# Turning the second half's normalised tokens on VectorE and through DRAM instead of on TensorE

## The chip, the core and the metric

One core of a Trainium2 chip. The metric is the device time of one execution in microseconds (us); the median of the runs is used. Engines, as the profile names them: PE is TensorE (PEld its weight loads), DVE is VectorE, ACT is ScalarE, POOL is GpSimd, SP is SyncE, whose queue (SPq) issues the DMAs.

## The reference

S = 2048 tokens of D = 576 values, all in 32 bits. `x` is normalised per token, and the result is the input plus the sum of two branches:

```python
xn = _layernorm(x)                       # (x - mean) / sqrt(var + 1e-5)
return x + A(xn, wqkv, wo) + B(xn, w1, b1, w2)
# A: 32 heads of 18; each token attends to itself and 7 earlier tokens, 2 apart; then @ wo
# B: h = xn @ w1 + b1; h * tanh(softplus(h)); @ w2      (576 -> 4608 -> 576)
```

## The kernel before, in words

**Halves, blocks, tiles.** The tokens are worked in two halves of 1024 (hf 0 and 1), each of two blocks (b 0 and 1), each of four tiles (jj) of 128 tokens. Tile n = 4 b + jj of a half holds 128 tokens that lie 8 apart, one per partition.

**Numbers in two parts.** Matmuls run on float32r. Every operand is split into a high part (a cast, on ScalarE) and a low part (the value minus the high part, on VectorE or POOL), and a product is made of three matmuls: high by high, high by low, low by high.

**Normalised and turned.** For a product over D the tokens must lie with D on the partitions. In the second half a tile goes this way: `x_load` (L103) loads it from `x` into a buffer of the tag "xn"; `norm1` (L137) normalises it in place on ScalarE and POOL copies the last 64 columns once more; `ln_transpose` (L184) saves a remainder `rem` on POOL and calls `transpose_split` (L67). That makes five transposes of 128x128 on TensorE into two PSUM banks (four L75, one L76; for block 1 a sixth of the remainder, L78). Then ScalarE casts the high parts out of the banks (L81, L86) and VectorE subtracts for the low parts (L82, L87). The result is `XTs[1, b]`, the turned tokens of the block. Three of the tiles take their banks from the tag "out" (`pair=True`), the others from "h". The statistics of these tiles are taken earlier (`stats1`, `root1`, `newton1`).

**Who uses it.** `qkv_item` (L327) makes q, k and v of one tile and a group of heads: 14 matmuls of 128x432 (L348), emptied by ScalarE (L350, L351). Groups 0 and 1 are done so; groups 2 and 3 by the items z (`z_part`, L446), which need sums `Ss` of the turned blocks (`s_step` on POOL, L620; `s_high`, `s_low`, L652 and L656). `m1_part` makes h and Mish of a quad q of 256 hidden units (L669, L675; `mish`, L715 to L721), `m2_pair` multiplies by w2 and VectorE adds to the sums `accs` in SBUF (L767, L771). After the last quad of the first half `y_store` (L1041) writes the sums of a chunk to DRAM, right after the chunk's item.

**Attention** is a background on POOL and VectorE: for each pair of head groups POOL multiplies q by k (`pr`, L533), VectorE reduces (L538) and makes the softmax (L548 to L564), POOL multiplies by v (`pv`, L571), VectorE reduces (`og`, L577) and turns the result in 32x32 blocks (`o_turn`, L593); four DMAs put it in DRAM so that the blocks come to lie turned (`o_send`, L602), and later loads find it fully turned.

**The order** is written out by hand. `plan` is a list of slots; a slot has one item of TensorE (`add`), and functions are hung in front of it (`before(i, fn)`). What is recorded is what each engine does, in that order: every engine, and SP's queue of DMAs, is strictly in order. Around the change the slots are: quads 15, 16 and 17 of the first half; then `t` of tile 3 (call that slot e), two chunks of the last quad, then q items of group 0 and the other two chunks in turn, with the `t` slots of tiles 4 to 7 between them.

**Buffers.** A tag with `bufs` buffers is given out in rotation; a new tile waits until the last user of the old one is done. DMAs signal on eight semaphores in rotation, so that a DMA also waits for the eighth one before it.

Of the kernel before, what the change touches and what calls it, by code (L numbers as in the profile page):

```python
# [8 lines left out]
F32 = mybir.dt.float32  # L9
# [8 lines left out]
P = 128  # L18
# [21 lines left out]
def block_kernel(ctx: ExitStack, tc: tile.TileContext, x, wq, wo, w1, b1, w2, mask, out):  # L40
# [23 lines left out]
    for k in range(30):  # L64
        nc.tensor.transpose(warm[:, (k % 4) * P:(k % 4 + 1) * P], ident, ident)

    def transpose_split(src, dst, col, extra=None, pair=False):  # L67
        n = next(tpn)
        if pair:
            ta, tb = (ps.tile([P, 512], F32, tag="out", bufs=4, name=f"tt{k}_{n}") for k in range(2))  # L70
        else:
            ta = ps.tile([P, 512], F32, tag="h", bufs=4, name=f"ta_{n}")
            tb = ps.tile([P, 512], F32, tag="h", bufs=4, name=f"tb_{n}")
        for k in range(KT):
            nc.tensor.transpose(ta[:, k * P:(k + 1) * P], src[:, k * P:(k + 1) * P], ident)  # L75
        nc.tensor.transpose(tb[:, 0:P], src[:, KT * P:(KT + 1) * P], ident)  # L76
        if extra is not None:
            nc.tensor.transpose(tb[:, P:2 * P], extra, ident)  # L78
        tav = ta.rearrange("p (k t) -> p k t", k=KT)
        hi = dst[:, 0:KT, col:col + P]  # L80
        nc.scalar.copy(hi, tav)  # L81
        nc.vector.tensor_sub(dst[:, 5:5 + KT, col:col + P], tav, hi.bitcast(F32))  # L82
# [4 lines left out]
        nc.vector.tensor_sub(hr[64:P], tbv[64:P], hr[64:P].bitcast(F32))  # L87
# [15 lines left out]
    def x_load(n):  # L103
        xn = sb.tile([P, 5 * P], F32, tag="xn", bufs=XNB, name=f"xn_1_{n}_{next(tpn)}")
        nc.sync.dma_start(xn[:, 0:D], x_tile(1, n))
        xns[1, n] = xn

# [76 lines left out]
    def ln_transpose(hf, b, jj):  # L184
# [10 lines left out]
        transpose_split(xn, XTs[hf, b], jj * P, rem if b else None, (hf, b) == (1, 0) and jj < 3)  # L195

    def raw_load(src, width, name):
        raw = sb.tile([P, 5 * P], F32, tag="raw", bufs=4, name=f"r{name}")
# [841 lines left out]
    def y_store(j):  # L1040
        nc.sync.dma_start(y_d.rearrange("(p j) d -> p j d", j=TJ)[:, j, :], accs[0][j])  # L1041
# [553 lines left out]
```

## Time and profile before

| what | us |
|---|---|
| runs | 1114.26, 1114.43, 1114.8 |
| median | 1114.43 |
| the profiled execution | 1114.25 |
| its span, first to last instruction | 1112.5 |
| PE busy | 1101.6 |
| POOL busy | 790.8 |
| DVE busy | 849.5 |
| ACT busy | 499.5 |

The granted TensorE clock was 1.000 over the span. How to read the views: a row of the timeline has the start, the duration, the engine, the line, what it writes and reads, and in square brackets how long the engine was idle before it and what it had been waiting for. A row of the windows has the stretch, then the busy time of PE, PEld, DVE, ACT and POOL, the clock, the busy share of the 16 DMA engines and what they moved in GB/s. A row of the groups has a line's operation with its count, the busy time and the mean ns. A row of the source view has the shortest, median and longest duration in ns. The chain of waits is followed back from the last instruction, and each piece is charged only what it added. Matmuls overlap on PE, so the busy time of one is longer than what it adds.

### The profile page before, as it was taken

The page shows a single profiled execution, that of the slowest core. Times are in us where ns is not written, and L with a number is a line of the kernel's source. Part 1 is how long each engine was busy: PE and PEld are TensorE (multiplying, and loading weights), DVE is VectorE, ACT ScalarE, POOL GpSimd, SP SyncE. Part 2 cuts the span into 40 slices and gives each one's busy share as a digit, 9 for nine tenths or more (in the row PEclk, how much of TensorE's full clock was granted, in tenths as well). Part 3 has the DMA queues.
Part 4 walks back from the last instruction along what each step waited for, and adds up shares of the span by engine and source line. Part 5 has one row for each costly group of instructions (what it writes and reads, how often), then busy time and mean ns, then how long its engine had stood idle before and what let it go on. Part 6 is the DMA issues. An engine that isn't in the chain of part 4 may idle for free.

```text
span 1112.5 us, 18203 instructions
## 1 busy us (share of the span) xinstructions
PE 1101.6 (99%) x6550; PEld 1015.2 (91%) x6550; DVE 849.5 (76%) x1367; ACT 499.5 (45%) x917; POOL 790.8 (71%) x639
## 2 busy tenths in 40 slices
PE   9999999999999999999999999999999999999998
PEld 8999899999999999999999889989989999999998
DVE  6369788888889888897656577786776677777786
ACT  5544655544454544555333354433433344343353
POOL 2479777766679688785788676666688976867532
PEclk9999999999999999999999999999999999999999
DMA  6899696868777758675597898565664657776574
GB/s 202 283 312 316 225 356 214 285 233 276 258 242 264 268 208 301 249 249 204 190 323 241 245 375 307 211 196 196 220 222 170 209 195 223 244 288 219 171 232 142
DMA packets 178270, 271.60 MB, mean 244 GB/s; under 512 B 53218, under 2 KB 120068, under 8 KB 178180
## 3 DMA queue, kind: packets, MB, share of 16 engines
q1 hardware_dynamic: 178180, 270.44, 71.6%
q8 instruction: 52, 0.85, 0.3%
q14 instruction: 38, 0.31, 0.1%
HBM read 160.39 MB, written 110.00 MB: 243 GB/s over the span
## 4 chain that ended last, share of the span: by engine, by line
PE 87%; POOL 6%; DVE 3%; issue 2%; ACT 1%; DMA 0%; SPq 0%; POOLq 0%; DVEq 0%; ACTq 0%
PE h L669 28%; PE po L767 21%; PE pq L348 9%; PE po L880 9%; PE po L859 6%; PE h L675 5%; PE o L1063 5%; PE z L446 3%; POOL pv L571 2%; POOL accP L868 1%; POOL pr L533 1%; POOL act L721 1%; POOL s L620 1%; DMA acc<-in_x 0%; PE ta L75 0%
## 5 line engine op out<-in xcount | busy, mean ns | idle before, releaser
L767 PEld LDWEIGHTS po<-w,act 128*128 128x128 f32 x1728 | 236.4, 188 | 6.0 <-POOL act L721 0.4
L767 PE MATMUL po<-w,act 128*128 128x288 f32 x1728 | 240.7, 295 | 0.1
L533 POOL TENSOR_TENSOR pr<-q,kv 128x576 f32<-128x576 f32 x128 | 196.9, 1563 | 8.5 <-DMA q<-q_d 5.0
L721 POOL TENSOR_TENSOR act<-c,act 128x512 fp32r<-128x512 f32 x81 | 107.3, 1325 | 128.6 <-ACT act L720 128.6
L571 POOL TENSOR_TENSOR pv<-L,kv 128x576 f32<-128x576 f32 x128 | 177.9, 1484 | 26.1 <-DVE L L564 21.2
L771 DVE TENSOR_TENSOR acc<-po,acc 128x288 f32<-128x288 f32 x288 | 119.4, 448 | 29.9 <-PE po L767 29.0
L348 PE MATMUL pq<-wq,xt 128*128 128x432 f32 x672 | 136.5, 361 | 1.0 <-ACT xt L81 1.0
L880 PEld LDWEIGHTS po<-w,act 128*128 128x128 f32 x960 | 130.9, 188 | 4.6 <-DVE accP L883 1.8
L880 PE MATMUL po<-w,act 128*128 128x288 f32 x960 | 133.5, 295 | 1.0 <-DVE accP L883 1.0
L348 PEld LDWEIGHTS pq<-wq,xt 128*128 128x128 f32 x672 | 125.0, 188 | 8.0 <-ACT xt L81 1.8
L715 ACT ACTIVATE c<-c,b1c 128x512 f32<-128x512 f32 x81 | 58.7, 725 | 140.7 <-DVE c L714 140.4
L669 PE MATMUL h<-xt,t 128*128 128x512 f32 x432 | 110.6, 391 | 0.5 <-DVE rt L714 0.3
L669 PE MATMUL h<-S,t 128*128 128x512 f32 x432 | 110.5, 391 | 0.0
L577 DVE TENSOR_REDUCE og<-pv 128x144 f32<-128x1152 f32 x64 | 86.0, 1345 | 25.7 <-POOL pv L571 25.6
L669 PE MATMUL h<-xt,wa 128*128 128x512 f32 x432 | 104.1, 390 | 0.0
L538 DVE TENSOR_REDUCE L<-pr 128x64 f32<-128x1152 f32 x64 | 85.8, 1341 | 23.8 <-POOL pr L533 23.7
L703 ACT COPY c<-h 128x512 f32<-128x512 f32 x81 | 47.4, 586 | 124.1 <-PE h L675 73.0
L859 PEld LDWEIGHTS po<-pw,u 128*128 128x128 f32 x672 | 92.2, 188 | 5.4 <-DVE u L813 2.1
L859 PE MATMUL po<-pw,u 128*128 128x288 f32 x672 | 94.3, 295 | 2.5 <-DVE u L813 1.6
L669 PEld LDWEIGHTS h<-xt,wa 128*128 128x128 f32 x432 | 80.9, 188 | 17.0
L669 PEld LDWEIGHTS h<-xt,t 128*128 128x128 f32 x432 | 79.0, 188 | 15.7 <-DVE rt L714 0.7
L883 DVE TENSOR_TENSOR accP<-po,accP 128x288 f32<-128x288 f32 x160 | 68.9, 452 | 29.8 <-PE po L880 28.2
(228 smaller groups left out, 1853.8 us busy)
## 6 DMA issues: line engine op xcount, KB each, us to landing
kv<-kv_d SPq DMA_DIRECT2D x64, 396.0 KB, 5.1
kept_t<-t SPq DMA_DIRECT2D x36, 512.0 KB, 4.8
t<-kept_t SPq DMA_DIRECT2D x36, 512.0 KB, 6.7
rw<-in_w SPq DMA_DIRECT2D x36, 320.0 KB, 4.4
kept_wa<-wa SPq DMA_DIRECT2D x18, 640.0 KB, 4.7
kept_w<-w SPq DMA_DIRECT2D x20, 576.0 KB, 4.1
wa<-kept_wa SPq DMA_DIRECT2D x18, 640.0 KB, 5.2
w<-kept_w SPq DMA_DIRECT2D x20, 576.0 KB, 4.1
```

The lines of the kernel that those rows point to most:

```text
L348: nc.tensor.matmul(pq[:, 0:432], XT[:, xi, tok], wt[wi][:, hl, 0:432], start=i == 0, stop=i == len(seq) - 1)
L533: nc.gpsimd.tensor_tensor(out=pr[:, x:x + hh], in0=q[:, j0 + x:j0 + x + hh, None, :].to_broadcast([P, hh, W, CU]), in1=win(kt, 0, CU, j0 + ...
L538: nc.vector.tensor_reduce(L[:, k, j0:j0 + hj].rearrange("p j w h -> p (j w h)"), pr.rearrange("p j w (h d) -> p (j w h) d", h=2), axis=AX, ...
L571: nc.gpsimd.tensor_tensor(out=pr[:, x:x + hj].rearrange("p j d w -> p j w d"), in0=L[:, k, x:x + hj, :, h:h + 1].to_broadcast([P, hj, W, DH]),
L577: nc.vector.tensor_reduce(og[:, c0:c0 + DH, :].rearrange("p d j -> p j d"), pr, axis=AX, op=ALU.add)
L669: nc.tensor.matmul(ph, wt[:, wl, wk * P:(wk + 1) * P], X[:, xs, :], start=first and i == 0, stop=last and i == len(seq) - 1, skip_group_ch ...
L721: nc.gpsimd.tensor_tensor(out=a[:, 1, :], in0=t, in1=a[:, 0, :].bitcast(F32), op=ALU.subtract)
L767: nc.tensor.matmul(po, acts[hf, q, b, j][:, al, tok], done["w2", hf, 2 * q + j][:, wl, c * HC:(c + 1) * HC], start=i == 0, stop=i == 5)
L771: nc.vector.tensor_tensor(out=t, in0=po, in1=t, op=ALU.add)
L859: nc.tensor.matmul(po, units[e, k, qq][:, al, tok], w[:, qq, wl, :], start=i == 0, stop=i == 5)
L880: nc.tensor.matmul(po, acts[hf, q, b, j][:, al, tok], done["w2", hf, 2 * q + j][:, wl, c * HC:(c + 1) * HC], start=i == 0, stop=i == 5)
L883: nc.vector.tensor_tensor(out=t, in0=po, in1=t, op=ALU.add)
```

## The change

For the second half's eight tiles the transposes of TensorE go. A tile is loaded and normalised earlier (tiles 4 to 7 into buffers of the tag "raw"), turned in 32x32 blocks by VectorE (`x_turn`), stored by four DMAs so that it lies fully turned in DRAM (`x_put`), and loaded back by three DMAs, the last 64 rows twice (`x_back`). `x_high` makes the remainder on POOL and the high parts on ScalarE, `x_low` the low parts on VectorE, both from the loaded tile in SBUF. For block 1 the remainder's two parts are operations of their own. POOL's copy of the last 64 columns goes. The slots are written out below. `y_store` of a chunk moves from the chunk's item to two slots later. Line numbers after the change are larger by 46 from `attention` on.

```diff
-    def transpose_split(src, dst, col, extra=None, pair=False):
+    def transpose_split(src, dst, col, extra=None):
...
+    def x_load(n, tag="xn"):
+        xn = sb.tile([P, 5 * P], F32, tag=tag, bufs=BUFS[tag], name=f"xn_1_{n}_{next(tpn)}")
...
     def norm1(n):
         xn = xns[1, n]
         nc.scalar.activation(xn[:, 0:D], xn[:, 0:D], AF.Identity, bias=nm1[:, n, :], scale=rs1[:, n, :])
-        nc.gpsimd.tensor_copy(xn[:, D:D + 64], xn[:, KT * P:D])
+
+    def x_turn(n):
+        if n == 0:
+            xTs["a"] = sb.tile([P, D], F32, tag="acc", bufs=9, name="xT_a")
+            xTs["b"] = sb.tile([P, 2 * 432], F32, tag="r3", bufs=1, name="xT_b")[:, 0:D]
+        t = xTs["ab"[n % 2]]
+        nc.vector.transpose(t, xns[1, n][:, 0:D])
+        xTs[n] = t
+
+    def x_put(n):
+        t = xTs[n]
+        d = xT_d[n] = dram.tile([D, P], F32, name=f"xT_d{n}")
+        rows = d.rearrange("(n i) p -> i n p", i=32)
+        for g in range(4):
+            part = slice(g * 32, (g + 1) * 32)
+            nc.sync.dma_start(rows[:, :, part], t[part].rearrange("i (n k) -> i n k", k=32))
+
+    def x_back(n):
+        xn = xns[1, n] = sb.tile([P, 5 * P], F32, tag="xn", bufs=XNB, name=f"xn_t_{n}")
+        nc.sync.dma_start(xn[:, 0:KT * P].rearrange("p (k t) -> p k t", k=KT),
+                          xT_d[n][0:KT * P].rearrange("(k p) t -> p k t", p=P))
+        for r_ in range(2):
+            nc.sync.dma_start(xn[r_ * 64:(r_ + 1) * 64, KT * P:], xT_d[n][KT * P:D])
+
+    def x_parts(n):
+        b, jj = divmod(n, JB)
+        cs = slice(jj * P, (jj + 1) * P)
+        xn, dst, rem = xns[1, n], XTs[1, b], rems[1][:, jj, :]
+        return [(xn[:, 0:KT * P].rearrange("p (k t) -> p k t", k=KT), dst[:, 0:KT, cs], dst[:, 5:5 + KT, cs]),
+                *((x_, dst[:, k, cs], dst[:, k, cs]) for x_, k in ((xn[:, KT * P:], KT), (rem, 9))[0:1 + b])]
+
+    def x_high(n):
...
+        if b == 0:
+            nc.gpsimd.tensor_copy(rem, xr)
+        else:
+            nc.gpsimd.tensor_tensor(out=rem, in0=rem, in1=xr, op=ALU.subtract)
+        for s_, hi, lo in x_parts(n):
+            nc.scalar.copy(hi, s_)
+
+    def x_low(n):
+        for k, (s_, hi, lo) in enumerate(x_parts(n)):
+            r_ = slice(64 if k else 0, P)
+            nc.vector.tensor_tensor(out=lo[r_], in0=s_[r_], in1=hi[r_].bitcast(F32), op=ALU.subtract)
...
     def pr_(hf, q, b, p, alias=None):
-        def end():
-            if hf == 0 and q == NP - 1:
-                for jj in (2 * p, 2 * p + 1):
-                    y_store(b * JB + jj)
-        add(("p", hf, q, b, p), lambda: ((m2_cols if hf else m2_pair)(hf, q, b, p), end()), alias=alias)
+        add(("p", hf, q, b, p), lambda: (m2_cols if hf else m2_pair)(hf, q, b, p), alias=alias)
...
     def tr(b, jj):
-        add(("t", 1, b, jj), lambda: ln_transpose(1, b, jj))
+        add(("t", 1, b, jj))
...
-    i = spot(0, NP - 2, 0)
-    for jj in range(JB):
-        before(i + 2 * jj, lambda jj=jj: x_load(jj))
-        before(i + 2 * jj + 6, lambda jj=jj: norm1(jj))
-        before(at["t", 1, 0, jj] + 2, lambda jj=jj: x_load(JB + jj))
-    for jj in range(JB):
-        before(at["p", 0, NP - 1, 1, 1] + jj, lambda jj=jj: norm1(JB + jj))
+    i, e = spot(0, NP - 3, 8), at["t", 1, 0, JB - 1]
+    for n in range(TJ):
+        b_, jj = divmod(n, JB)
+        turn = (e - 7, e - 4, e - 1, e + 2)[jj] if b_ else i + 3 * jj + 3
+        load_at = (e - 13, e - 12, e - 10, e - 6)[jj] if b_ else i + 3 * jj
+        split = e + (8, 10, 12, 13)[jj] if b_ else e + (-5, -2, 1, 4)[jj]
+        before(load_at, lambda n=n: x_load(n, "raw" if n >= JB else "xn"))
+        before(turn - 1, lambda n=n: norm1(n))
+        before(turn, lambda n=n: x_turn(n))
+        before(turn + 2, lambda n=n: x_put(n))
+        before(e + (3, 5, 7, 8)[jj] if b_ else split - 5, lambda n=n: x_back(n))
+        before(split, lambda n=n: x_high(n))
+        before(split + 1, lambda n=n: x_low(n))
...
+    for n, (b, p) in enumerate(CHUNKS):
+        for jj in (2 * p, 2 * p + 1):
+            before(at["p", 0, NP - 1, b, p] + 2, lambda j=b * JB + jj: y_store(j))
```

The q item of tile n stands at e + (3, 5, 8, 10, 12, 14, 15, 16)[n], the chunks of the last quad at e + 1, e + 2, e + 4 and e + 6. VectorE's order from the last of these chunks on is now: the turn of pair 5's attention output, the reduce of pair 6's first pr, the lows of tiles 4 and 5, a reduce, the lows of tiles 6 and 7, two reduces, the mask and the softmax, the lows of S.

More of the change, by code (lines that the diff above doesn't have):

```diff
@@ L65, in block_kernel @@
         nc.tensor.transpose(warm[:, (k % 4) * P:(k % 4 + 1) * P], ident, ident)
-    def transpose_split(src, dst, col, extra=None, pair=False):
+    def transpose_split(src, dst, col, extra=None):
         n = next(tpn)
[L69 to L73, printed above, removed]
+        ta = ps.tile([P, 512], F32, tag="h", bufs=4, name=f"ta_{n}")
+        tb = ps.tile([P, 512], F32, tag="h", bufs=4, name=f"tb_{n}")
         for k in range(KT):
@@ L101, in x_tile @@
         return x[hf * SH:(hf + 1) * SH, :].rearrange("(p j) d -> p j d", j=TJ)[:, n, :]
-    def x_load(n):
-        xn = sb.tile([P, 5 * P], F32, tag="xn", bufs=XNB, name=f"xn_1_{n}_{next(tpn)}")
+    def x_load(n, tag="xn"):
+        xn = sb.tile([P, 5 * P], F32, tag=tag, bufs=BUFS[tag], name=f"xn_1_{n}_{next(tpn)}")
         nc.sync.dma_start(xn[:, 0:D], x_tile(1, n))
@@ L139, in norm1 @@
         nc.scalar.activation(xn[:, 0:D], xn[:, 0:D], AF.Identity, bias=nm1[:, n, :], scale=rs1[:, n, :])
-        nc.gpsimd.tensor_copy(xn[:, D:D + 64], xn[:, KT * P:D])
+    def x_turn(n):
[25 more added lines that the diff above has]
+    def x_high(n):
+        b, jj = divmod(n, JB)
+        if jj == 0:
+            XTs[1, b] = sb.tile([P, 9 + b, TB], F32R, tag=f"xt{b}", bufs=1, name=f"xt_1_{b}")
+        if n == 0:
+            rems[1] = sb.tile([P, JB, P], F32, tag="tt", bufs=2, name="rem_1")
+        rem, xr = rems[1][:, jj, :], xns[1, n][:, KT * P:]
+        if b == 0:
[8 more added lines that the diff above has]
+            nc.vector.tensor_tensor(out=lo[r_], in0=s_[r_], in1=hi[r_].bitcast(F32), op=ALU.subtract)
+    xT_d, xTs = {}, {}
     group = {}
@@ L194, in ln_transpose @@
             nc.gpsimd.tensor_tensor(out=rem, in0=rem, in1=xn[:, KT * P:], op=ALU.subtract)
-        transpose_split(xn, XTs[hf, b], jj * P, rem if b else None, (hf, b) == (1, 0) and jj < 3)
+        transpose_split(xn, XTs[hf, b], jj * P, rem if b else None)
     def raw_load(src, width, name):
```

## The prediction

> **What bounds the kernel now.** I read the page first, then the busy times by stretch, then the chain of work that ended last around the place where the change sits.
>
> ```profile
> span 1112.5 us, 18203 instructions
> PE 1101.6 (99%) x6550; PEld 1015.2 (91%) x6550; DVE 849.5 (76%) x1367; ACT 499.5 (45%) x917; POOL 790.8 (71%) x639
> 470.00:565.00 95.00, 95.00 (x587) 89.05 (x587) 75.09 (x113) 41.77 (x79) 70.71 (x66) 1.00 0.67 231
> ```
>
> TensorE is busy 99% of the span, and in the 95 us in which the second half's tokens are normalised and turned it never idles (95.00 of 95.00). What leaves its list there shortens the program at once, as long as nothing else becomes late. The chain a little later says how little room there is:
>
> ```profile
> 571.27 2.95 POOL pv L571 x2
> ...
> 588.90 2.98 POOL pv L571 x2
> ...
> 591.91 1.36 DVE og L577
> ...
> 594.65 0.37 DVE zkv L459
> 595.02 0.23 DVE zqs L459
> ...
> 595.29 29.75 PE z L446 x150
> ```
>
> From 571 to 592 us the chain runs over POOL (attention pair 6, first half of the tokens, with the sums of the second half between), from there over VectorE, and TensorE's product z of tile 0, part 3, starts when VectorE has emptied its bank. So POOL's first pv of pair 6, at 571.2 us, already decides when TensorE goes on at 595.3 us. The reader should keep that pair of times: whatever delays the first passes on to the second one for one.
>
> **What is removed.** The groups of TensorE between 512 and 557 us:
>
> ```profile
> L75 PE MATMUL ta<-ident,xn 128*128 128x128 f32 x20 | 3.0, 272 | 0.0
> L75 PE MATMUL tt<-ident,xn 128*128 128x128 f32 x12 | 1.8, 272 | 0.0
> L76 PE MATMUL tb<-ident,xn 128*128 128x128 f32 x5 | 1.4, 273 | 0.0
> L78 PE MATMUL tb<-ident,rem 128*128 128x128 f32 x4 | 1.1, 272 | 0.0
> L76 PE MATMUL tt<-ident,xn 128*128 128x128 f32 x3 | 0.8, 273 | 0.0
> 545.66 0.44 PE ta L75 x4
> 546.10 0.11 PE tb L76
> ```
>
> That is 20 + 12 + 5 + 4 + 3 = 44 transposes. Matmuls overlap, so the 272 ns of one are not its price: the chain charges 0.44 us for four and 0.11 us for one. 44 x 0.11 = **4.84 us** off TensorE: 2.20 us before the half's first q item (20 transposes), 0.66 us ahead of each of four later items. In the built program TensorE's list is otherwise unchanged in content and order, so the change does what it says. Eight small POOL copies (L140) go too; no step here waits for them.
>
> **What is added on queues, and what hides it.** Eight turns on VectorE, each with four stores into DRAM and three loads back: 32 + 24 DMAs, issued by SP. The attention outputs already take the same road:
>
> ```profile
> L593 DVE STREAM_TRANSPOSE oT<-og x16: 759/778/781, 141.0 to 1049.8; 128x576 f32<-128x576 f32 x16
> L602 SPq DMA_DIRECT2D o_d<-oT x72: 303/507/1478, 143.1 to 1054.4; - x72
> DMA to landing us min/median/max: 1.9/2.4/5.2
> ```
>
> ```profile
> 548.00:549.00 1.00, 1.00 (x7) 0.90 (x6) 1.00 (x1) 0.00 (x0) 0.00 (x0) 1.00 0.88 135
> SPq L1041 <- DVE acc L771: 15.1, 8, 4.0
> 554.00:596.00 42.00, 41.87 (x216) 39.64 (x215) 27.51 (x31) 14.85 (x41) 37.17 (x28) 1.00 1.01 331
> ```
>
> The turn has the shape of the kernel's oT turn, 0.78 us always. A put has the shape of the o_d stores: 0.51 us of SP's queue for each of the four, 288 KB at 135 GB/s = 2.2 us of the DMA engines. Eight puts take 17.6 us of DMA and 16 us of SP; the loads back, about 320 KB a tile, I put at 1.0 us of the DMA engines and 1.5 us of SP: at the 331 GB/s of a full stretch (554 to 596 us), their runs being 512 bytes; at a put's rate they would take 2.5 us. The DMA engines were 0.67 busy over these 95 us, so 31 us are free, and 26 are asked for (38 at the worse rate). SP gets room back: it waited 15.1 us for the sums in front of the eight y_d stores, and two slots later it finds them ready. What queues behind a waiting put is V, K and weight loads with 10 us or more of lead, and each tile's data are back 5 to 15 us ahead of its item. So I take **0** for transfers, with 2 us as the upper end (the last loads of wq and those of z meet DMA engines that are full from 554 us on, and two y_d stores and a load back now stand ahead of them: 3 x 0.9 us, less what gaps take up), and 0 for ScalarE, 41.77 us busy in 95.
>
> By the Trainium skill's page "VectorE: DVE Perf Modes", section "The three transpose paths", a plain DMA copy that turns data by its access pattern is 19 times slower than the proper path; by that an estimate of 17 us a put (19 x 0.89) would stand for the measured 2.2. Here only 32x32 blocks are carried, in runs of 128 bytes, and the row of the o_d stores decides against it.
>
> **What is added on VectorE: inputs from SBUF.** Until now the low part of a tile was made from a PSUM bank. Now both inputs lie in SBUF, and tiles 4 to 7 need three operations instead of two (12 instead of 8). Rows for the two kinds:
>
> ```profile
> L82 DVE TENSOR_TENSOR xt<-ta,xt x13: 681/691/692, 9.5 to 557.1; 128x512 fp32r<-128x512 f32 x13
> L87 DVE TENSOR_TENSOR xt<-tt,xt x3: 294/294/295, 515.1 to 526.8; 64x128 fp32r<-64x128 f32 x3
> L656 DVE TENSOR_TENSOR S<-s,S x12: 649/1766/1923, 58.3 to 594.0; 128x512 fp32r<-128x512 f32 x12
> L548 DVE TENSOR_TENSOR L<-L,mk x8: 411/414/1248, 86.1 to 611.8; 2x256 f32<-2x256 f32 x8
> 559.21 2.67 POOL L620 TENSOR_TENSOR s<-s,xt 128x512 f32<-128x512 f32 x2
> 560.91 1.25 DVE L548 TENSOR_TENSOR L<-L,mk 2x256 f32<-2x256 f32 x1
> ```
>
> From PSUM 128x512 is 0.68 to 0.69 us, whatever POOL does. From SBUF (S) it is 0.65 us at best and 1.77 us in the median. Even the mask's 2x256, 0.41 us alone, took 1.25 us at 560.91: it lasted until POOL's second s operation was over (559.21 + 2.67 = 561.88) plus its own 0.3. So such an operation waits for the POOL instruction under way, however small it is itself, and 1.766 - 0.649 = **1.12 us** is the price of a block.
>
> By the Trainium skill, "SBUF — State Buffer", section "Who interferes with whom", a VectorE instruction with two SBUF inputs and a GpSimd instruction that reads SBUF exclude each other for the whole instruction. By it a block could last a whole POOL operation, 1.3 us, and nine of them 1.6 us more than below, which an estimate would put at 1118.8 us; the median row is nearer.
>
> **First place: the half's first sum.** The item p of chunk (1,0) of the last quad needs act of block 34:
>
> ```profile
> 520.86 2.55 POOL L571 TENSOR_TENSOR pv<-L,kv 128x576 f32<-128x576 f32 x2 [0.36 <-PE h L669]
> 521.74 0.69 DVE L714 TENSOR_TENSOR c<-h,c 128x512 f32<-128x512 f32 x1
> 522.47 0.73 ACT L715 ACTIVATE c<-c,b1c 128x512 f32<-128x512 f32 x1 [2.36 <-DVE c L714]
> 523.93 1.29 POOL L721 TENSOR_TENSOR act<-c,act 128x512 fp32r<-128x512 f32 x1 [0.40 <-ACT act L720]
> 527.15 6.61 PE L767 MATMUL po<-w,act 128*128 128x288 f32 x48
> ```
>
> Before, the act was ready at 525.22 and wanted at 527.15. Now TensorE is there at 524.95, and in front of the c addition VectorE has tile 0's two low operations, which alternate with POOL's copy (0.3) and first pv half (1.3), and a turn: 0.3 + 0.65 + 1.3 + 0.3 + 0.78 = 3.3 us where 0.97 stood; the rest of its queue is there 0.55 earlier: +1.8 us. The act is ready at 527.0; the third matmul wants it at 525.2. **Stall 1.85 us**; 0 if nothing collides.
>
> **Second place: from the last sum to pair 6's first pv.** VectorE's order there is: turn oT, reduce L, lows of tiles 4 and 5, reduce, lows of 6 and 7, two reduces, mask, S. Before:
>
> ```profile
> 546.07 0.77 DVE L593 STREAM_TRANSPOSE oT<-og 128x576 f32<-128x576 f32 x1
> 547.48 0.43 DVE L87 TENSOR_TENSOR xt<-tb,xt 64x256 fp32r<-64x256 f32 x1
> 550.22 0.69 DVE L82 TENSOR_TENSOR xt<-ta,xt 128x512 fp32r<-128x512 f32 x1 [0.93 <-ACT xt L81]
> 553.64 0.69 DVE L82 TENSOR_TENSOR xt<-ta,xt 128x512 fp32r<-128x512 f32 x1 [2.27 <-ACT xt L81]
> 557.08 0.69 DVE L82 TENSOR_TENSOR xt<-ta,xt 128x512 fp32r<-128x512 f32 x1 [0.90 <-ACT xt L81]
> 567.77 0.69 DVE L656 TENSOR_TENSOR S<-s,S 128x512 fp32r<-128x512 f32 x1 [2.47 <-ACT S L652]
> ```
>
> The chain is taken against these rows:
> 1. Start: TensorE 2.20 earlier, less the 1.85 us stall: -0.35.
> 2. Lows before: 4 x (0.69 + 0.43) = 4.47, and 0.93 + 2.27 + 0.90 = 4.10 of waiting for ScalarE behind TensorE's turns: 8.57. Now 4 x 0.65 + 8 x 0.294 = 4.95 alone. POOL's queue there is two pr, the remainders, the s operations, back to back: I place the 12 one by one against them, alternating, and find 9 that meet a running POOL operation, 3 (the first of tiles 4, 5 and 6) that do not: 9 x 1.12 = 10.1. Together 15.0, or +6.4.
> 3. Behind them: the mask alone 0.41 instead of 1.25 (-0.84), and the 2.47 us for which VectorE waited for ScalarE's S go, since VectorE is now the later: -3.3.
> Sum **+2.8 us** for pair 6's first pv, and so for z at 595 us: all of the 4.84 us is waited away there, and 2.8 more. On the way TensorE also waits about 2.6 us for tile 7's low part at its item; that time lies inside the sum, not on top. After 597 us POOL idles, so the shift stays as it is to the end.
>
> **The sum.** The profiled execution took 1114.25 us (span 1112.5 and 1.75 around it): 1117.05. The median of the runs shown is 0.18 above it: **1117.2 us**. With n blocked operations the sum is 2.8 + 1.12 x (n - 9); n = 7 to 12 gives 1114.9 to 1120.6, this case's own range.
>
> **Rivals.**
> - *POOL seldom in the way* (n of 4 or less). Then TensorE sets the pace again and gets most of its 4.84 us: 1109.6 with no stall at all, 1110.5 with half of the first one. For it: a tile's data are there early, and POOL idles where it waits for VectorE. Against: POOL is busy 37.17 of the 42 us from 554 on. It decides from n below 6.5, where the sum passes zero.
> - *Balance*, n of 5 or 6: 1112.7 to 1113.8, no change.
> - *Transfers late*: n small, but the 2 us of DMA lag eat into the gain: 1114.4 - 4.84 + 2.0 = 1111.6.
> - *Strided stores slow*: puts that follow each other at the o_d stores' longest landing, 5.2 us, want 8 x 5.2 + 8 x 1.5 = 54 us of the 31 that are free; 23 us late, less 4.84: 1132. Against: the median landing of 2.4, and 135 GB/s. The page named above would make it later still.
>
> **How the numbers follow.** Forecast 0.53, of which 0.40 slower by over 0.2% (2.2 us, about what a measurement of this kernel can tell from no change) and 0.13 within; balance 0.15 within; POOL seldom in the way 0.23 faster; transfers 0.05 faster; strided stores 0.04 slower. Faster 0.28, same 0.28, slower 0.44. The range from 1110.0 to 1120.0 leaves out about 2 in 10: the far ends of the first rival and of the forecast, and the last rival.
>
> **What would show it.** Right: TensorE's busy time 4.8 us lower in total; lows of xt from SBUF at 1.3 to 1.9 us (128x512) and over 1 us (64x128) between 545 and 565 us; an idle gap of TensorE at the first sum, at tile 7's item, and one of several us ahead of z, with VectorE named; pair 6's first pv at about 574 us. Wrong: lows near 0.7 us, that pv at 567 us or earlier, no gap ahead of z. A put over 3 us, or TensorE waiting for a DMA, would move the blame to transfers.

## The result, and the profile after

The changed kernel took 1118.45 us in the median of 6 runs (1117.49 to 1119.08), the kernel before 1114.52 (1114.23 to 1114.80): a ratio of 1.0033, with a 95% interval of 1.0023 to 1.0043. It is 3.9 us slower. The profiled execution took 1118.23 us, 1116.4 of them span.

The page's totals, and the busy times of the 95 us in which the change sits (columns as in the row shown of before: PE, PEld, DVE, ACT, POOL, granted clock, DMA share, GB/s):

```profile
span 1116.4 us, 18214 instructions
PE 1098.9 (98%) x6506; PEld 1009.8 (90%) x6506; DVE 859.9 (77%) x1379; ACT 501.2 (45%) x921; POOL 793.9 (71%) x631
470.00:565.00 95.00, 91.66 (x545) 84.44 (x543) 82.22 (x121) 43.72 (x85) 68.33 (x55) 1.00 0.91 264
```

The 44 transposes are gone (6550 less 6506 matmuls), and TensorE, which never idled here, now idles 3.34 us. The DMA engines went from 0.67 to 0.91. What TensorE and POOL wait for, from the views of waits (total, times, longest):

```profile
PE pq L394 <- DMA wq<-kept_wq: 3.7, 5, 1.1
PE po L813 <- POOL act L767: 0.8, 1, 0.8
```

```profile
POOL rem L178 <- DMA xn_t<-xT_d: 5.2, 2, 4.7
POOL rem L176 <- DMA xn_t<-xT_d: 2.4, 1, 2.4
```

None of the three rows that name a DMA has a counterpart in the kernel before. POOL's timeline shows where its wait sits:

```profile
552.85 0.47 POOL L178 TENSOR_TENSOR rem<-rem,xn_t 128x128 f32<-128x128 f32 x1 [4.70 <-DMA xn_t<-xT_d]
553.27 3.28 POOL L579 TENSOR_TENSOR pr<-q,kv 128x576 f32<-128x576 f32 x2
574.83 3.00 POOL L617 TENSOR_TENSOR pv<-L,kv 128x576 f32<-128x576 f32 x2
```

The small remainder of tile 6 stands in POOL's queue in front of the third row of pair 6's pr, and waits 4.70 us for the tile's load back. In the kernel before the same pr has this line:

```profile
549.37 2.83 POOL L533 TENSOR_TENSOR pr<-q,kv 128x576 f32<-128x576 f32 x2 [1.78 <-DVE L L538]
```

It starts 3.90 us later now. From there to pair 6's first pv it is 21.6 us now and was 21.9: nothing more is lost on that stretch. And TensorE's z of tile 0, part 3:

```profile
598.85 1.46 PE L492 MATMUL z<-z_B,S 128*128 128x432 f32 x6 [0.82 <-DVE zqs L505]
```

It was 595.29, so 3.56 us later, for a pv that is 3.60 later: the pair of times that the forecast told the reader to keep moved together.

Why the load was late is on SP's queue (start, us for all, count):

```profile
515.82 4.38 SPq L152 DMA_DIRECT2D xT_d<-xT_a  x4
...
524.65 4.03 SPq L152 DMA_DIRECT2D xT_d<-xT_b  x4
...
529.80 0.38 SPq L328 DMA_DIRECT2D wq<-kept_wq  x1
...
531.95 0.53 SPq L328 DMA_DIRECT2D wq<-kept_wq  x1
532.57 3.35 SPq L152 DMA_DIRECT2D xT_d<-xT_a  x4
...
540.33 2.21 SPq L152 DMA_DIRECT2D xT_d<-xT_b  x4
...
547.32 0.50 SPq L156 DMA_DIRECT2D xn_t<-xT_d  x1
```

The four rows of L152 are the puts of tiles 4, 5, 6 and 7. All eight puts hold SP for 26.1 us, where the forecast took 16. In the built program each DMA of SP waits for the one that was issued eight before it, whatever the two have to do with each other: a put for a weight load, in the first row below. But those waits are the smaller part, 1.6 and 0.6 us in the view of waits. The put of tile 5 met none of them; its third store alone took 2.06 us to issue (second row), where the o_d stores had 0.51 in the median.

```profile
SPq L152 <- DMA wq<-kept_wq: 1.6, 3, 1.1
525.77 2.06 SPq L152 DMA_DIRECT2D xT_d<-xT_b  x1
```

Why an issue took longer no run shows. What the rows do show is that SP was nearly full: from 515 to 556 us its issues take 35.1 of the 41 us (57 DMAs, 0.62 us each), and in the kernel before 13.4 (28 DMAs, 0.48 each). What stands behind a put is late with it. The two weight loads at 529.80 and 531.95 had these rows before:

```profile
520.84 0.32 SPq L282 DMA_DIRECT2D wq<-kept_wq  x1
526.88 0.32 SPq L282 DMA_DIRECT2D wq<-kept_wq  x1
```

Tile 6's put had been issued by 535.9, but its load back (547.32) stands behind tile 7's put, the loads back of tiles 4 and 5, six y_d stores and a load of V and K.

The view of DMAs from 480 to 566 us gives the time from issue to landing (median, last column), in the kernel before and, in the second block, in the changed one:

```profile
wq<-kept_wq SPq DMA_DIRECT2D x10, 432.0 KB, 4.1
```

```profile
wq<-kept_wq SPq DMA_DIRECT2D x10, 432.0 KB, 5.7
xT_d<-xT_a SPq DMA_DIRECT2D x16, 72.0 KB, 4.9
```

Last, the low parts of tiles 4 to 7 on VectorE, grouped by shape from 546 to 561 us (sum, mean ns of one):

```profile
L185 DVE TENSOR_TENSOR xt<-xn_t,xt 128x512 fp32r<-128x512 f32 x4 | 4.5, 1134 | 0.6 <-ACT xt L180 0.6
L185 DVE TENSOR_TENSOR xt<-xn_t,xt 64x128 fp32r<-64x128 f32 x4 | 3.3, 813 | 0.1
L185 DVE TENSOR_TENSOR xt<-rem,xt 64x128 fp32r<-64x128 f32 x4 | 1.4, 352 | 0.0
```

That is 9.2 us where the forecast has 15.0. Operations of tiles 6 and 7 meet POOL's as forecast (2.93 and 2.98 us for a 128x512 and a 64x128 that take 0.95 alone); those of tiles 4 and 5 do not (1.00 and 1.01), for POOL was itself waiting for loads.

So there were two explanations to tell apart, and a third limit to watch. *Loads hold POOL*: late transfers set the end. *Locks* (the forecast's): low parts with two inputs from SBUF set it. *Late weights*: TensorE's 3.7 us of waiting for wq.

### The profile page after: what moved, and what is told of

It is laid out like the page before. It is cut to its first block, busy times and chain, and to the rows that moved or that the text cites. A ratio compares the mean times of both kernels' runs of the same rounds, so it can differ in the third digit from the quotient of the medians.

```text
span 1116.4 us, 18214 instructions
## 1 busy us (share of the span) xinstructions
PE 1098.9 (98%) x6506; PEld 1009.8 (90%) x6506; DVE 859.9 (77%) x1379; ACT 501.2 (45%) x921; POOL 793.9 (71%) x631
## 4 chain that ended last, share of the span: by engine, by line
PE 81%; POOL 8%; DVE 4%; DMA 2%; issue 2%; ACT 1%; SPq 0%; POOLq 0%; DVEq 0%; ACTq 0%
PE h L715 27%; PE po L813 19%; PE po L926 9%; PE pq L394 7%; PE po L905 6%; PE h L721 5%; PE o L1109 5%; PE z L492 3%; POOL pv L617 2%; POOL pr L579 2%; POOL accP L914 1%; POOL s L666 1%; POOL act L767 1%; DMA t<-kept_t 1%; DMA xn_t<-xT_d 1%
## 5 line engine op out<-in xcount | busy, mean ns | idle before, releaser
L617 POOL TENSOR_TENSOR pv<-L,kv 128x576 f32<-128x576 f32 x128 | 179.5, 1498 | 25.8 <-DVE L L610 21.3
L817 DVE TENSOR_TENSOR acc<-po,acc 128x288 f32<-128x288 f32 x288 | 119.1, 449 | 25.1 <-PE po L813 24.1
L584 DVE TENSOR_REDUCE L<-pr 128x64 f32<-128x1152 f32 x64 | 85.9, 1342 | 28.5 <-POOL pr L579 28.4
```

What stands on the lines that cost most here:

```text
L584: nc.vector.tensor_reduce(L[:, k, j0:j0 + hj].rearrange("p j w h -> p (j w h)"), pr.rearrange("p j w (h d) -> p (j w h) d", h=2), axis=AX, ...
L617: nc.gpsimd.tensor_tensor(out=pr[:, x:x + hj].rearrange("p j d w -> p j w d"), in0=L[:, k, x:x + hj, :, h:h + 1].to_broadcast([P, hj, W, DH]),
L817: nc.vector.tensor_tensor(out=t, in0=po, in1=t, op=ALU.add)
```

## The experiments

Each median stands against runs of the kernel before on the same chip.

### Loads back earlier

```
-        before(e + (3, 5, 7, 8)[jj] if b_ else split - 5, lambda n=n: x_back(n))
+        before(e + (3, 4, 4, 6)[jj] if b_ else split - 5, lambda n=n: x_back(n))
```

> The changed kernel with one thing moved: the loads back of tiles 5, 6 and 7 are issued 1, 3 and 2 slots earlier, so that on SP they stand ahead of the put of tile 7, the y_d stores and the loads of V and K that now precede them. Theory *loads hold POOL*: in the changed kernel POOL's remainders of tiles 3, 5 and 6 waited 2.35, 0.46 and 4.70 us for loads back, and everything from pair 6's pr to its first pv (574.83 us) stood behind them; so POOL's wait for tile 6 should fall below 1 us, that pv should come at 570 to 572 us and the time at 1114.0 to 1116.0 us. Theory *locks* (the forecast's): what sets that pv is VectorE's low parts with two inputs from SBUF; they stay, so pv stays at 574 to 575 and the time at 1118 to 1119. Theory *late weights*: TensorE's 3.7 us of waiting for wq decide; they stay about as they are, and so does the time.

Median 1117.05 us (1115.70 to 1122.19), ratio 1.0029 [1.0015, 1.0042]. Its profile:

```profile
545.01 0.89 POOL L178 TENSOR_TENSOR rem<-rem,xn_t 128x128 f32<-128x128 f32 x2
572.19 3.01 POOL L617 TENSOR_TENSOR pv<-L,kv 128x576 f32<-128x576 f32 x2
561.01 3.80 PE L394 MATMUL pq<-wq,xt 128*128 128x432 f32 x18 [1.56 <-DVE xt L185]
```

POOL no longer waits for tile 6, and pair 6's first pv comes 2.64 us earlier: *loads hold POOL* was right about this place. But now the low parts of all four tiles meet a busy POOL. The same groups in this kernel:

```profile
L185 DVE TENSOR_TENSOR xt<-xn_t,xt 128x512 fp32r<-128x512 f32 x4 | 3.9, 964 | 0.1
L185 DVE TENSOR_TENSOR xt<-xn_t,xt 64x128 fp32r<-64x128 f32 x4 | 5.4, 1340 | 0.1
L185 DVE TENSOR_TENSOR xt<-rem,xt 64x128 fp32r<-64x128 f32 x4 | 4.7, 1180 | 0.0
```

They sum to 14.0 us; the forecast had 15.0. It is the small ones that pay: 1.2 to 1.3 us in the mean where 0.29 is their time alone. And the wait of TensorE for tile 7's low part, which the forecast put at 2.6 us and the changed kernel did not have, is here with 1.56. The time moved by 1.4 us only, which the two intervals don't tell from nothing; it missed the 1114 to 1116 that was expected. Two of the eight runs, 1119.16 and 1122.19 us, had a mean granted clock of 0.998 and 0.995; the other six had 1.000.

### Low parts from PSUM

```
         for s_, hi, lo in x_parts(n):
             nc.scalar.copy(hi, s_)
+            nc.scalar.copy(t, s_)        # t: a bank of PSUM, which x_low then reads in place of s_
```

> The changed kernel, but ScalarE also copies each loaded tile into PSUM (two banks a tile, as the transposes used to fill), and VectorE makes the low part from there: one input from SBUF, one from PSUM. ScalarE gets about 20 copies more (some 8 us of the 60 it has free there); what the low parts mean is unchanged. Theory *locks*: the low parts of tiles 6 and 7 (2.93 + 2.98 + 0.55 + 0.28 us in the changed kernel) fall to about 2 us in all and the four of tiles 0 to 3 from 8.4 to about 4, so pair 6's first pv comes 2 to 4 us earlier and the time is 1114.5 to 1116.5 us. Theory *loads hold POOL*: the remainder of tile 6 still waits 4 to 5 us for its load, pv stays at 574 to 575 us and the time at 1117.5 to 1119.

Median 1117.22 us, ratio 1.0024 [1.0015, 1.0034]. The low parts cost 0.69 us for 128x512 and 0.29 for 64x128 again, whatever POOL does. POOL's waits for loads stay:

```profile
552.51 0.46 POOL L178 TENSOR_TENSOR rem<-rem,xn_t 128x128 f32<-128x128 f32 x1 [4.29 <-DMA o_d<-oT]
573.36 3.02 POOL L623 TENSOR_TENSOR pv<-L,kv 128x576 f32<-128x576 f32 x2
```

pv is 1.5 us earlier, less than *locks* wanted (2 to 4), more than *loads hold POOL* (0). Neither alone carries the loss.

### Half of the tiles each way

Tiles 0 to 3 through DRAM and 4 to 7 on TensorE, and the other way round:

```
-        add(("t", 1, b, jj))
+        add(("t", 1, b, jj), *([] if b in (0,) else [lambda: ln_transpose(1, b, jj)]))
...
+        if b_ not in (0,):
+            (x_load and norm1 of tile n at the slots of the kernel before)
+            continue
```

In these two kernels the block difference, POOL's remainder of tiles 4 to 7, subtracts a tile that is turned from one that is not, so that part is not what the reference computes; the instructions and their sizes are the same.

> Only tiles 0 to 3 go through DRAM; tiles 4 to 7 are turned on TensorE as before (24 transposes, 2.64 us, stay; 20, 2.20 us, go). The y_d stores stay two slots later. Theory *loads hold POOL*: no load back of tiles 4 to 7 exists, so POOL's remainders there wait for nothing; what is left is the stall at the half's first sum (about 1.1 us) and perhaps the load back of tile 3 in front of pair 5's last pv (2.35 us); pair 6's first pv at 570 to 572 us, the time 1113.0 to 1115.0 us. Theory *locks*: the same place is free of locks too, so this run alone does not tell the two apart; it gives the price of the first place, at most +1.9 - 2.2 = -0.3 us against the kernel before by the forecast: 1114.2. Theory *late weights*: four puts fewer stand in front of wq 5 to 9, so TensorE's waits for wq fall from 3.7 us to below 2.

Median 1112.75 us, ratio 0.9985 [0.9975, 0.9994]: 1.8 us faster than the kernel before, of the 2.20 that 20 transposes are worth. Both edges of its profile:

```profile
525.63 6.38 PE L816 MATMUL po<-w,act 128*128 128x288 f32 x46 [0.24 <-POOL act L770]
569.40 2.99 POOL L620 TENSOR_TENSOR pv<-L,kv 128x576 f32<-128x576 f32 x2
```

The stall at the half's first sum is 0.24 us, and TensorE waits for no weight at all.

> Only tiles 4 to 7 go through DRAM; tiles 0 to 3 are turned on TensorE as before (20 transposes stay, 24, 2.64 us, go). The y_d stores stay two slots later. Theory *loads hold POOL*: four puts fewer stand ahead on SP, but tile 6's load back keeps its place behind the y_d stores, tile 7's put and the V and K load; POOL's wait for it shrinks to 1 to 4 us, pv at 571 to 574 us and the time 1114.5 to 1117.5 us, in step with that wait. Theory *locks*: the low parts of tiles 4 to 7 keep their 9 to 15 us, the first place costs nothing, and pv comes 2 to 4 us later than in the kernel before whatever POOL's wait for the load is: 1116.5 to 1118.5 us.

Median 1115.76 us, ratio 1.0012 [1.0002, 1.0021]: 1.2 us slower.

```profile
POOL rem L181 <- DMA xn_t<-xT_d: 3.8, 2, 2.7
```

```profile
572.09 3.02 POOL L620 TENSOR_TENSOR pv<-L,kv 128x576 f32<-128x576 f32 x2
```

POOL still waits 3.8 us for loads, and the low parts of the four tiles sum to 13.0 us. pv came 0.86 us later than before; this and the median lie in the windows of the first theory and below those of the second.

The sum of the two halves is -1.8 + 1.2 = -0.6 us; the whole change is +3.9. So 4.5 us arise only when all eight tiles go at once. The locks of tiles 4 to 7 are not what is added, for their low parts took less in the whole (9.2 us) than in the half (13.0). What the halves share is SP's queue (its issues take 28.4 and 36.7 of the 55 us from 505 to 560, and 47.8 with both) and the DMA engines (0.83 and 0.81 busy from 470 to 565 us, 0.91 with both). TensorE's wait for wq is 0 and 0.4 us in the halves and 3.7 in the whole.

### The transfers alone

The kernel before, with 32 stores from a constant tile and 24 loads into a scratch tile at the changed kernel's slots, and the later y_d stores (`turn` and `split` as in the change):

```
+        before(turn + 2, lambda n=n: x_put(n))
+        before(e + (3, 5, 7, 8)[jj] if b_ else split - 5, lambda n=n: x_back(n))
```

> The kernel before with the change's 56 transfers added at the changed kernel's slots and nothing else of it but the later y_d stores: the stores come from one constant tile, what is loaded back goes to a scratch tile that nobody reads. All 44 transposes stay; no turn, no low part from SBUF, no wait of POOL for a load back. It gives the price of the transfers by themselves, which the forecast put at 0 with 2 us as the upper end. Theory *transfers delay the weights*: TensorE waits 2 to 4 us for wq in front of q items, and the time is 1116 to 1118 us. Theory *only waiting for the loads back hurts*: 1114.3 to 1115.3 us, TensorE's waits for wq below 1 us.

Median 1119.60 us, ratio 1.0046 [1.0031, 1.0061]: **5.2 us**, above what either theory gave. Its view of waits, and two lines of its timelines:

```profile
PE pq L370 <- DMA wq<-kept_wq: 4.0, 2, 2.7
```

```profile
540.41 0.78 PE L370 MATMUL pq<-wq,xt 128*128 128x432 f32 x2 [2.74 <-DMA wq<-kept_wq]
577.27 3.00 POOL L593 TENSOR_TENSOR pv<-L,kv 128x576 f32<-128x576 f32 x2
```

Nobody reads these transfers, and no transpose or low part changed. SP is as full as in the changed kernel: its issues take 46.9 of the 55 us from 505 to 560, there 47.8. TensorE still waits 4.0 us for wq 2 and wq 4 of the half's first q item, and everything behind it is 6.05 us late in this execution. (The rest is mostly clock: see the last section.)

### The stores of the sums alone

```
-                for jj in (2 * p, 2 * p + 1):
-                    y_store(b * JB + jj)
+            before(at["p", 0, NP - 1, b, p] + 2, lambda j=b * JB + jj: y_store(j))
```

> The kernel before with one part of the change: the stores of the sums two slots later, nothing else. The forecast took this part at nothing. *Nothing*: within 0.5 us of the kernel before, and SP's wait in front of the y_d stores (15.1 us) falls to below 3. *It makes later loads late*: wq 5 to 9 and the loads of z come 1 to 3 us later behind the two stores, and the time rises by 0.5 to 2 us. *It helps*: the loads of V and K and of wq that stood behind those waits come earlier, 0.5 to 1 us off.

Median 1114.79 us, ratio 1.0003 [0.9993, 1.0012]: nothing, as the forecast had it. But SP still waits for sums,

```profile
SPq L1041 <- DVE acc L771: 9.8, 6, 3.8
```

9.8 us where 15.1 stood and below 3 was expected. Where nothing is added, that wait costs nothing either way.

### The puts on ScalarE's queue

```
-            nc.sync.dma_start(rows[:, :, part], t[part]...)
+            nc.scalar.dma_start(rows[:, :, part], t[part]...)
```

> The changed kernel with its 32 stores of turned tiles issued by ScalarE instead of SP: the same transfers, bytes and runs, another queue. Theory *order on SP's queue* (each DMA waits there for what stands ahead of it): the loads back and wq 2, 4 and 5 to 9 are issued 5 to 10 us earlier, POOL waits under 1 us for loads, TensorE under 1 us for wq, and the time is 1114 to 1117 us (locks stay), if ScalarE's own copies do not get late by it. Theory *the DMA engines are too slow for these stores*: loads back and wq land as late as before, 1117.5 to 1119 us. Rival: ScalarE is held by the stores it must wait for, its copies (kvs, act, high parts) get late, and the time is over 1119.

Median 1125.88 us, ratio 1.0096 [1.0079, 1.0112]. The rival: ScalarE is held. Its views of waits, and TensorE's line at the half's first sum:

```profile
ACT xn L136 <- DMA xT_d<-xT_a: 5.7, 1, 5.7
POOL rem L178 <- DMA xn_t<-xT_d: 2.3, 2, 1.7
SPq L245 <- DMA xT_d<-xT_a: 1.7, 1, 1.7
```

```profile
534.09 0.85 PE L813 MATMUL po<-w,act 128*128 128x288 f32 x2 [4.22 <-DVE acc L817]
```

The stores' waits hold activations. One normalisation waits 5.7 us, VectorE and POOL stand behind it, and TensorE waits 4.22 us at the first sum alone. TensorE no longer waits for wq, and POOL's remainders of tiles 4 to 7 wait 2.3 us for loads instead of 5.2. That does not show that the loads came earlier: wq 2 and wq 4 were issued at 530.32 and 532.43, 0.5 us later than in the changed kernel, but the half's first q item began at 543.49 instead of 532.71. Nor were the two queues free of each other. In the trace the 32 stores carry the same eight semaphores as SP's DMAs, in one rotation, and SP waits for them, as in the last row of the waits, where a load of weights waits for a store of a tile. By the Trainium skill's page "DMA: Bandwidth & Descriptors", section "Issuing engines are not separate DMA queues", starting DMAs on several engines saves only the time that it takes to start them, since the same 16 engines carry them all. This run agrees as far as it can tell: a second queue brought no gain.

### Both limits away, then all three

The first two edits together:

> The two edits together: loads back of tiles 5 to 7 earlier, and the low parts made from a copy in PSUM. Theory *two limits, the later one counts*: with the loads early pair 6's first pv came at 572.2 us and locked low parts were then in front of it; with low parts from PSUM alone it came at 573.4 and the load of tile 6 was; with both gone it should come at 568 to 570 us, TensorE should reach z without a wait for zqs, and the time should be 1111 to 1114 us, more than the two single gains (1.4 and 1.2 us) together. Theory *additive*: the single gains add up, 1118.4 - 2.6 = 1115.8 us. Theory *late weights*: TensorE still waits some 3 us for wq, and the time stays above 1115.

Median 1116.95 us, ratio 1.0020 [1.0011, 1.0030]. The expected 1111 to 1114 is missed, and so is the sum of the single gains. The third limit took over:

```profile
PE pq L400 <- DMA wq<-kept_wq: 4.1, 4, 2.0
```

TensorE reaches z without waiting for zqs, as expected, but 4.1 us of waiting for weights are in front of it. So the weights were put first:

```
-        before(at["q", 1, 0, 0, 3] + k, lambda k=k: fetch("wq", 5 + k))
+        before(at["q", 1, 0, 0, 3] - 1, lambda k=k: fetch("wq", 5 + k))
-        turn = (e - 7, e - 4, e - 1, e + 2)[jj] if b_ else i + 3 * jj + 3
+        turn = (e - 7, e - 4, e - 1, e + 3)[jj] if b_ else i + 3 * jj + 3
-        before(turn + 2, lambda n=n: x_put(n))
+        before(e + 1 if n == 5 else turn + 2, lambda n=n: x_put(n))
-            before(at["p", 0, NP - 1, b, p] + 2, lambda j=b * JB + jj: y_store(j))
+            before(at["p", 0, NP - 1, b, p] + (2 if b else 8), lambda j=b * JB + jj: y_store(j))
```

> The kernel with early loads back and low parts from PSUM, and on SP also the weights put first: tile 5's put behind wq 4, tile 7's turn and put a slot later, wq 5 to 9 in one go a slot before their old place, the last four y_d stores behind them. Theory *three limits, the latest counts* (loads back, locks, late weights): TensorE's waits for wq fall from 4.1 us to below 1.5, and only now does the 4.84 us of removed transposes show: 1111 to 1114 us. Rival, *there is not enough transfer time*: eight in flight and engines that are 0.97 busy from 480 to 520 and 547 to 566 us just make something else late (K and V, loads of z, the q_d store that a sum on POOL waits for): 1115 to 1118 us.

Median 1117.64 us, ratio 1.0029 [1.0020, 1.0039].

```profile
569.58 2.99 POOL L623 TENSOR_TENSOR pv<-L,kv 128x576 f32<-128x576 f32 x2
576.30 1.29 POOL L672 TENSOR_TENSOR s<-xt 128x512 f32<-128x512 f32 x1 [3.74 <-DMA q_d<-qs]
588.02 0.66 PE L498 MATMUL z<-z_R,xt 128*128 128x432 f32 x2 [1.48 <-DMA z_R<-kept_wq]
```

Now no weight is late, no lock is met, and pair 6's first pv comes at 569.58, 5.25 us before that of the changed kernel. The loss has moved behind it: a sum on POOL waits 3.74 us for the store of q whose buffer it takes, and TensorE waits for loads of z. The rival held: with all 56 transfers, something on SP's ordered queue was late in each of the arrangements tried.

### A version that is faster than both

Tiles 0 to 3 through DRAM, 4 to 7 on TensorE, with the block difference taken after the turn, so that four more transposes go. Its high and low parts (x_rest) were placed in three ways:

```
+        if extra is not None and e == 1:
+            nc.vector.tensor_tensor(out=extra, in0=extra, in1=tb[:, 0:P], op=ALU.subtract)
...
+            before(e + 20 + jj, lambda jj=jj: x_rest(jj))       # then e + 14 + jj // 2, then e + 18 + jj
```

With the third place the remainders also move from the buffer of the tag "tt", which a load of z takes over, to that of "r3".

> Tiles 0 to 3 through DRAM, tiles 4 to 7 on TensorE, and the block difference taken after the turn: VectorE subtracts the transposed bank from the loaded remainder, so four more transposes go (24 of 44 in all, 2.64 us), and the high and low of that difference are made eight to ten slots later. The kernel with tiles 0 to 3 alone took 1112.75 us with 20 gone; *loads and locks at the second place were the loss*: 1112.0 to 1113.2 us here, under the kernel before by 1.3 to 2.5, with pair 6's first pv at 569 to 570 us. If the four added VectorE operations hold L's sums or S up: 1113.5 to 1115.

Median 1126.31 us, ratio 1.0100 [1.0085, 1.0115]. pv came at 568.86, as expected, and the time 12 us late. SP's timeline and TensorE's waits:

```profile
557.98 23.06 SPq L476 DMA_DIRECT2D ztt_T<-kept_T  x2
```

```profile
PE z L505 <- DMA zacc_B<-kept_wq: 4.8, 4, 2.6
```

The remainders now held their buffer longer, the first load of z that wanted it kept SP for 23 us, and every load behind it came late. One release on an ordered queue cost more than the whole change.

> The kernel called mixed with its four late high and low parts of the block difference made six slots earlier, before the first load of z that wants the buffer of the remainders. In mixed SP waited at that load until 580.4 us, and the loads of z stood behind it (TensorE waited 9.5 us for them). Theory *one held buffer on SP's ordered queue was the 12 us*: TensorE no longer waits for loads of z, pair 6's first pv stays at about 569 us, and the time is 1111.8 to 1113.2 us, at or under that of tiles 0 to 3 alone (1112.75), because four more transposes (0.44 us) are gone. Rival, *the extra VectorE operations cost what the transposes save*: 1113.2 to 1114.6.

Median 1113.30 us, ratio 0.9990 [0.9981, 1.0000]. The 12 us are gone; VectorE's added operations now stand in front of S, and POOL waits 2.27 us there.

> Tiles 0 to 3 through DRAM, tiles 4 to 7 on TensorE, the remainders in a buffer that no load of z wants early, and the high and low of the block difference made behind VectorE's S of the first sum (in the last version they stood in front of it, and POOL waited 2.27 us for that S). 24 of the 44 transposes are gone (2.64 us), 28 transfers are added instead of 56. Theory *the transfers behind 530 us and what waits for them were the loss, the first four tiles are nearly free*: pair 6's first pv at 568.5 to 570 us, TensorE waits for no weight and no load of z, and the time is 1112.0 to 1113.0 us, 1.4 to 2.4 below the kernel before. Rival: VectorE's operations behind S delay og and zqs, TensorE waits over 1 us at z, and nothing is won over the last version: 1113.0 to 1114.0.

Median 1112.34 us (11 runs), ratio 0.9983 [0.9974, 0.9992]: 2.0 us faster than the kernel before, and about 6 faster than the changed one.

```profile
569.34 2.57 POOL L630 TENSOR_TENSOR pv<-L,kv 128x576 f32<-128x576 f32 x2
593.48 1.45 PE L505 MATMUL z<-z_B,S 128*128 128x432 f32 x6 [0.32 <-DVE zqs L518]
```

24 transposes (2.64 us) are gone, 28 transfers are added, no weight is late, and 2.0 of the 2.64 us arrive at the end.

The main kernels side by side. The waits and the two starts come from one profiled execution each, the last column from the medians, in us. The intervals of the last column reach 1.0 to 1.7 us to each side, so the five kernels from +2.3 to +3.9 are told apart by their traces, not by their times. Of the 9.2 in one row, 4.3 stand in a row that names an o_d store.

| kernel | transfers added | POOL waits for loads back | TensorE waits for wq | pair 6's first pv | z, tile 0, part 3 | against before |
|---|---|---|---|---|---|---|
| before | 0 | 0 | 0 | 571.23 | 595.29 | |
| changed | 56 | 7.6 | 3.7 | 574.83 | 598.85 | +3.9 |
| loads back earlier | 56 | 0.5 | 1.1 | 572.19 | 596.28 | +2.5 |
| low parts from PSUM | 56 | 9.2 | 3.4 | 573.36 | 597.48 | +2.7 |
| both | 56 | 3.9 | 4.1 | 572.72 | 598.49 | +2.3 |
| both, weights first | 56 | 2.8 | 0 | 569.58 | 597.35 | +3.2 |
| transfers alone | 56 | none reads | 4.0 | 577.27 | 601.34 | +5.2 |
| tiles 0 to 3 | 28 | 0 | 0 | 569.40 | 593.46 | -1.8 |
| tiles 4 to 7 | 28 | 3.8 | 0.4 | 572.09 | 596.12 | +1.2 |
| the last version | 28 | 0 | 0 | 569.34 | 593.48 | -2.0 |

## Why the prediction was right in its number and wrong in its cause

- **What bounds the kernel: right.** pv of pair 6 and z of tile 0, part 3, stand 24.0 to 24.1 us apart in all rows of the table but two. With both edits TensorE itself had become late (25.8), and with the weights first POOL waited between the two (27.8).
- **What is removed: right in count and worth.** The half with 20 fewer transposes gains 1.8 of 2.20 us, the last version 2.0 of 2.64. TensorE's busy time fell by 2.7 us, not by 4.8: by an estimate 1.6 of the missing 2.1 is the lower clock described below, and the rest I cannot place.
- **Transfers at 0, with 2 us as the upper end: the step that failed.** By themselves they cost 5.2 us. Their work was sized rightly: 26 us of the DMA engines were asked for, and from 470 to 640 us, a stretch that also holds the loads that were pushed back, their share rose from 0.75 to 0.90, which is about 25 of the 170 us. What failed are the two sentences about time in hand. "What queues behind a waiting put is V, K and weight loads with 10 us or more of lead" did not hold for wq 2 and wq 4, which stood behind the put of tile 5. "Each tile's data are back 5 to 15 us ahead of its item" looked at TensorE's items; but the first to want the data is POOL's remainder, slots earlier, and with it pair 6's pr. The margin was worked out from shares of busy time, where it had to come from the order on SP, DMA by DMA. SP's own time, 16 us for puts and 12 for loads back, was sized but never set against what SP had there: from 505 to 560 us its issues took 18.8 of the 55 us before and 47.8 after. The forecast's own marks for blame on transfers, a put over 3 us and TensorE waiting for a DMA, both showed.
- **The price of locks: right in sum, but only with the loads on time.** Then the low parts of tiles 4 to 7 took 14.0 us (forecast 15.0), and TensorE's wait for tile 7 appeared. Even then it was the 64x128 that paid; a 128x512 took 0.96 us in the mean, below the 1.3 to 1.9 of the forecast. In the changed kernel the low parts took 9.2 us, because POOL was waiting for loads and so not in the way. Late loads and locks stand in for each other there; that is why a sum that left out the first came out near the truth (pv at 574.0 expected, 574.83 measured). So the nearness of the number is luck: where the locks fell short by 5.8 us there stood waits for loads, 4.70 us in front of pair 6's third pr alone, that the sum had at nothing. By the Trainium skill, "SBUF — State Buffer", section "Who interferes with whom", a VectorE instruction with two SBUF inputs contends with a GpSimd instruction that reads SBUF, for a port pair that is an exclusive lock; a 64x128 of 0.29 us alone took 1.2 to 1.3 us in the mean with early loads, so the runs agree.
- **The stall at the first sum: too dear.** 1.85 us forecast, 0.83 of waiting measured, 0.24 in the half with tiles 0 to 3.
- **The y_d stores: right**, +0.1 us alone.
- **The rivals.** *Transfers late* was the right mechanism with the wrong size and sign: priced at 2 us against a gain of 4.84, it cost 5.2 by itself. *Strided stores slow* had the landing right (half of the stores took 4.9 us in the median, near its 5.2), not the 23 us of lag. The forecast's estimate of 17 us a put was not met by any: 4.38 us of SP's queue was the longest, and its stores landed in 5.1 us at most where the trace has their landing. *POOL seldom in the way* half happened (the six operations of tiles 4 and 5 met no POOL operation), and gained nothing, since POOL was out of the way only while it waited.

What stays open: how the 4.5 us that the two halves do not have split between the order on a nearly full SP and the fuller DMA engines, which may also be why an issue took 0.62 us instead of 0.48. The run with the puts on ScalarE's queue was to tell them apart, and could not: ScalarE's own waits made everything late, and the two queues still waited for each other.

## What to carry to other kernels

A transfer that is added costs what it pushes back: write out the issuing queue in order, with the time that each issue takes and the one eight before it that it waits for, and check the time in hand of every load behind it against its first reader, which may be a small operation on an engine that you were not looking at. A busy share of 0.67 says how much work fits, not when it lands. Where an edit removes one limit and little happens, look for the limit right behind it before you give the cause up; here three lay within 3 us of one another, and halving the change beat mending it.

## What the runs showed of the hardware that was not expected

TensorE's granted clock was halved for 3.4 us after it had waited. In the changed kernel three waits of 1.13, 0.21 and 0.53 us lie between 564.3 and 567.9 us. Three stretches of 1 us from there on (the clock is the third number from the end):

```profile
567.00:568.00 1.00, 0.47 (x3) 0.15 (x1) 0.93 (x3) 0.00 (x0) 1.00 (x1) 0.79 1.03 396
568.00:569.00 1.00, 1.00 (x3) 0.73 (x4) 1.00 (x2) 0.36 (x2) 0.92 (x2) 0.50 1.07 404
571.00:572.00 1.00, 1.00 (x7) 0.95 (x6) 0.93 (x3) 0.00 (x0) 1.00 (x1) 1.00 1.15 306
```

The trace has the clock at 0.50 from 567.58 to 570.99 us and at 1.00 on both sides. TensorE was busy for 3.1 of these 3.4 us, so an estimate of what it lost is half of that, 1.6 us. The time hardly depended on it: two of the six runs of the changed kernel had a mean clock of 1.000 and took 1117.49 and 1118.84 us. In the kernel with the transfers alone the clock was 0.50 from 540.80 to 544.22 us, behind its waits of 1.28 and 2.74 us. There 24 matmuls of one line took 4.80 us, and 24 more of the same line took 3.35 at 548.36; with the 4.0 of waiting that makes 5.5 of the 6.05 us by which it was late. In the 3.4 us before it fell TensorE had idled 1.6 us in the changed kernel and 2.7 in that one. In the kernel with early loads back, waits of 1.56, 0.17, 0.20 and 0.22 us between 559 and 567 us left it at 1.00 in the profiled execution. With the puts on ScalarE's queue it was halved for 3.4 and for 6.8 us, and in the first place of x_rest for 13.7. By the Trainium skill's page "TensorE: Matmul & The Clock Gate", part 1, the clock is halved after an idle window of about 3.4 us; here the half is as it says, but in the changed kernel and in the one with the transfers alone no single wait was that long, and the clock fell.
